# A rank-one term seeded into PSUM by ScalarE, and the doubling of P moved from VectorE to ScalarE

## The chip, the cores and the metric

The kernel runs on one core of a Trainium2 chip. The metric is the device time of one execution in microseconds (us). The time before is 1906.95 us, the median of three runs (1909.23, 1906.95 and 1906.66). The profiled execution took 1907.31 us, with a span of 1905.5 us from the first to the last instruction and a mean granted TensorE clock of 0.999.

## The reference

Two operations follow each other. First an input `x` of 8 x 3008 x 256 is mixed by a two-dimensional Fourier transform, of which the real part is kept. Then the 24,064 rows of 256 go through a two-layer network with a gelu in its quick form:

```python
X = np.fft.fft(np.fft.fft(x, axis=1), axis=2).real      # 8 x 3008 x 256
h = X.reshape(24064, 256) @ w_in                          # 256 x 2048
g = h * (1.0 / (1.0 + np.exp(-1.702 * h)))
out = g @ w_out                                           # 2048 x 256
```

## The kernel before, in words

**The mathematics of a step.** The transform over the 256 columns is folded into the first weights, so that TensorE forms the hidden layer from two real matrices, the cosine part and the sine part of the transform over rows. Two rows of the transform that mirror each other share them: with P the product with the cosine weights (`wcs[0]`), Q' that with the sine weights (`wcs[1]`) and N a rank-one term (a weight per hidden unit, `af2`, times a row of the transform that stands in `nb` on all partitions), the forward rows are N + P + Q' and the mirrored ones N + P - Q'. Row 0 of the sine operands holds the data of N, so the sine product as it stands in the kernel before is Q = Q' + N. `af2` is twice the weights' row, so `af2` times `nb` is 2N.

**Tiling.** The rows of a batch are handled in three blocks, each with two halves (`hh`) of 256 columns, of which the second half of the first block has 226. For each half, eight steps (`p` = 0 to 7, `NP` = 8) go through the 2,048 hidden units, 256 in a step. `steps` has 8 x 3 x 2 x 8 = 384 steps, of 48 in a batch. The first eight (`t < NP`) go by `hidden` and `rows` and are called the forward steps here; the other 376 go by the loop's second branch. The schedule is written out by hand: the loop at L915 to L977 gives the order in which each engine's queue gets its instructions, and `extra` (L869 to L913) puts the next batch's transform (`fold1` on GpSimd, `mix1` and `stage2` on TensorE, their evacuations, loads and stores) into certain steps.

**A step t of the 376.** `x` is one bank of PSUM, `b0` or `b1` in turn.

1. TensorE: `second(t)` adds Q to x (L532); P was put there a step earlier by `begin(t)` (L525). Each is four matmul calls in two column halves and leaves eight records in the profile.
2. TensorE: `product(t - LAG, 0)` and `product(t - LAG, 1)` (L640) multiply the activated rows of three steps ago (`LAG` = 3) by the second weights and add them up in the banks `po`, over the eight steps of a half. Between the two parts stands `begin(t + 1)`, the P of the next step. At the first step of a half (`(t - LAG) % NP == 0`) P comes ahead of all products. The products are of a Strassen-Winograd form: their operands are sums `s` of activated rows (`sums`, L566: two on GpSimd, L576 and L577, two on VectorE, L579 and L580), and one of the products is divided once more (`small_products`, L605, with sums by `deeper`, L586).
3. ScalarE: `middle(t + 2)` writes the rank-one term 2N to an SBUF tile `g` as two activations with a scale per partition (L544). `forward(t)` reads x and writes the gelu of the forward rows (L557). `activate_back(t - 1)` applies the gelu to the mirrored rows of the step before (L564).
4. VectorE: `doubled(t + 1)` reads x of the next step while it holds P alone, and makes g = 2P + 2N (L550). Q of that step may be added only after that. `backward(t)` forms g - x = N + P - Q' in reversed order (L505 in `reversed_sum`).
5. VectorE and ScalarE: every eighth step, `combine`, `combine_small`, `swap` and `combine_last` evacuate the po banks (L699, L705, L708, L728, L736 to L738, L747), transpose (L679) and store.

`spare` lists the PSUM banks that `bank` hands out. In the 376 steps it holds `b{t % 2}` (the bank of x of step t, free after the reversed subtraction) and `b2`; `mix1` and `stage2` take two banks from it. `mix1`'s evacuation is two ScalarE copies (L235), that of `stage2` four VectorE transposes (L340).

Of the kernel before, what the change touches and what calls it, by code (L numbers as in the profile page):

```python
# [43 lines left out]
LAG = 3  # L44
# [67 lines left out]
def kernel(ctx: ExitStack, tc, x, w_in, w_out, tab1, tab2, out):  # L112
# [31 lines left out]
    af2 = const.tile([128, NF], F32, tag="af2", name="af2")  # L144
# [65 lines left out]
    def mix1(b, m):  # L210

        ps = [bank("ps1") for _ in range(2)]
        queues = {}
        for i in (2 * m, 2 * m + 1):
            for r in range(2):
                for c in range(2):
                    rows, o = slice(64 * r, 64 * r + NA), ps[r][64 * c:64 * c + 64, i % 2 * D:(i % 2 + 1) * D]
                    jj, todo = 4 * i + 2 * r + c, queues.setdefault((r, c), [])
                    if jj:
                        todo.append((2, o, mat(w1, jj, rows), xt[rows, 31 - (2 * i + c), :], True, True))  # L220
                        continue
                    for k, c0, c1 in ((0, 0, H + 1), (1, H + 1, D)):
                        for part in range(2):
                            todo.append((1, o[:, c0:c1], mat(w1, ENDS[k + 2 * part], rows), e0[b][:, part, c0:c1], part == 0,
                                         part == 1))

        had = {key: 0 for key in queues}
        while any(queues.values()):
            key = min((key for key in queues if queues[key]), key=lambda key: (had[key], key))
            size, o, w, rhs, first, end = queues[key].pop(0)  # L230
            had[key] += size
            nc.tensor.matmul(o, lhsT=w, rhs=rhs, start=first, stop=end)  # L232

        for r in range(2):
            nc.scalar.copy(free(xt[:], (4 * m + r) * D, [2 * D, 2], [1, D]), free(ps[r][:], 0, [D, 2], [1, D]))  # L235
# [87 lines left out]
    def stage2(b, blk):  # L323
# [5 lines left out]
        for cs in range(2):  # L329
            for h in range(2):  # L330
                for g in range(4):
                    for u in range(NU):
                        rows, at = slice(64 * u, 64 * u + 64), cs * 256 + h * 128
                        nc.tensor.matmul(ps[u][32 * g:32 * g + 32, at:at + 128], lhsT=m[rows, cs, h * RUN:(h + 1) * RUN],  # L334
                                         rhs=t4[rows, 4 * blk:4 * blk + 4, cs * H + 32 * g:cs * H + 32 * g + 32],
                                         start=True, stop=True)
# [119 lines left out]
    def first_row(n):  # L456
# [4 lines left out]
        nc.scalar.copy(af2[:, 4 * n:4 * n + 4], ps[:, 4 * n:4 * n + 4])  # L461

# [24 lines left out]
    def hidden(t):  # L487

        n = width(t)
        pa, pb = bank("pa"), bank("pb")  # L490
        for ps, cs in ((pa, 0), (pb, 1)):
            for i in range(2):
                halves(ps[:, i * 256:i * 256 + n], *operands(t, cs, i), start=True, stop=True)
# [31 lines left out]
    def begin(t):  # L525

        n = width(t)
        x = xb[t] = bank("x", f"b{t % 2}")
        for i in range(2):
            halves(x[:, i * 256:i * 256 + n], *operands(t, 0, i), start=(i == 0), stop=False)  # L530

    def second(t):  # L532
        n = width(t)
        for i in range(2):
            halves(xb[t][:, i * 256:i * 256 + n], *operands(t, 1, i), start=False, stop=True)

    def middle(t):
# [3 lines left out]
        g = gt[t] = sp.tile([128, 512], F32, tag="dif" if t % 2 else "v", name="g")  # L541
        for i in range(2):
            f = 2 * p + i
            nc.scalar.activation(g[:, i * 256:i * 256 + n], nbt[b, blk][:, hh * 256:hh * 256 + n], ACTF.Copy,  # L544
                                 scale=af2[:, f:f + 1])

    def doubled(t):
        n = width(t)
        g = two(gt[t][:], n)
        nc.vector.scalar_tensor_tensor(g, two(xb[t][:], n), 2.0, g, op0=ALU.mult, op1=ALU.add)  # L550
# [89 lines left out]
    def product(t, part):  # L640

        p, n = steps[t][3], width(t)
        if part == 0 and p == 0:
# [16 lines left out]
        todo = plan[:2] if part == 0 else plan[2:]  # L660

        if t >= len(steps) - 2:
            if part == 0:
# [9 lines left out]
        if part and p == 0:  # L673
# [241 lines left out]
    for t in range(n + LAG):  # L915
        if t < NP:
            if t == NP - 2:
                spare[:] = [tag for tag in spare if tag[0] == "o"] + ["b2"]
            hidden(t)
            if t == NP - 1:  # L920
                begin(NP)
            if t == 0:
# [5 lines left out]
            if t >= LAG:  # L928
                for part in range(2):
                    product(t - LAG, part)  # L930
# [5 lines left out]
            if t == NP - 1:  # L936
                for ahead in range(2):
                    middle(NP + ahead)
        else:
            if t < n:  # L940
                if t + 2 < n:
                    middle(t + 2)
                second(t)
            heads = [(product, t - LAG, 0)] + [(begin, t + 1)] * (t + 1 < n)
            for fn, *args in heads[::-1] if t >= NP + LAG and (t - LAG) % NP == 0 else heads:
                fn(*args)
            product(t - LAG, 1)
            small_products(t - LAG, (1, 2, 4, 7))
            small_products(t - LAG - 1, (5, 6, 3))
            if t == NP:  # L950
                activate(t - 1)
            if t < n:
                forward(t)
            if NP < t <= n:
                activate_back(t - 1)
                sums(t - 1, nc.gpsimd)
# [3 lines left out]
        if NP <= t + 1 < n:  # L960
            doubled(t + 1)
        if t >= NP:
# [11 lines left out]
        if t >= NP:  # L974
            spare[:] = [f"b{t % 2}", "b2"]
# [30 lines left out]
```

## Time and profile before

| engine | busy us | share of the span |
|---|---|---|
| TensorE, matmuls | 1881.4 | 99% |
| VectorE | 1540.6 | 81% |
| ScalarE | 877.5 | 46% |
| GpSimd | 789.9 | 41% |

| what | line | count | busy us |
|---|---|---|---|
| P and Q, all matmuls into x | L480 | 6,016 | 766.2 |
| 2N by ScalarE | L544 | 752 | 336.6 |
| 2P + 2N by VectorE | L550 | 376 | 254.9 |
| reversed rows by VectorE | L505 | 440 | 255.9 |
| gelu of the forward rows | L557 | 376 | 221.9 |
| gelu of the mirrored rows | L564 | 376 | 231.5 |

Busy time is the time in which an engine had at least one instruction at work. A matmul's end is modelled and matmuls overlap, so that TensorE's busy time has to be checked against the starts of its matmuls. In the lines of the timeline, the columns are the start in us from the span's start, the duration in us, the engine (PE is TensorE, PEld its weight loads, DVE VectorE, ACT ScalarE, POOL GpSimd, SP the queue of SyncE), the source line, the operation, what it writes and reads, its shape and how many were merged. Square brackets hold the engine's idle time just before it, and who ended it.

### The profile page before, as it was taken

Reading aid. Unit: us, or ns where it says so; the run is one execution under the profiler, and the core shown is the slowest. Engines: PE = TensorE matmul, PEld = TensorE weight load, DVE = VectorE, ACT = ScalarE, POOL = GpSimd, SP = SyncE. Lnnn points to the kernel's source line nnn. Section 1 sums busy time; section 2 is a strip of 40 time slices with the busy share of each in tenths; the row PEclk is TensorE's granted clock in tenths of the full one; section 3 lists DMA queues with packets and bytes.
Section 4 is the critical chain, followed back from the end, with each engine's and each line's share of the span. In section 5 each row is a group of like instructions: output and inputs, shape, how many; then the busy total and the mean of one; then the engine's idle time right before and its main releaser. Section 6 shows DMA issues by size and latency. Waiting matters only on the chain.

```text
span 1905.5 us, 51020 instructions
## 1 busy us (share of the span) xinstructions
PE 1881.4 (99%) x21392; PEld 1360.9 (71%) x21392; DVE 1540.6 (81%) x3011; ACT 877.5 (46%) x1868; POOL 789.9 (41%) x1073
## 2 busy tenths in 40 slices
PE   8999999999999999999999999999999999999998
PEld 5666777777777777777777777777777767777775
DVE  7688878887788877897788878888787888778876
ACT  6644444454445444444444444444444444444442
POOL 4585324643246322563225532365223643233222
PEclk9999999999999999999999999999999999999999
DMA  8732351236221452315513163132720231202201
GB/s 272 176 50 17 90 82 14 49 52 119 18 23 40 71 101 18 51 22 102 63 15 57 22 117 44 22 53 44 113 25 20 18 50 49 27 14 17 27 13 23
DMA packets 145398, 104.92 MB, mean 55 GB/s; under 512 B 104914, under 2 KB 127986, under 8 KB 143984
## 3 DMA queue, kind: packets, MB, share of 16 engines
q1 hardware_dynamic: 143952, 101.14, 31.2%
q8 instruction: 167, 2.74, 0.6%
q10 hardware_dynamic: 1216, 0.52, 0.1%
q14 instruction: 63, 0.52, 0.1%
HBM read 58.38 MB, written 48.01 MB: 56 GB/s over the span
## 4 chain that ended last, share of the span: by engine, by line
PE 88%; DVE 8%; ACT 1%; DMA 1%; issue 1%; POOL 0%; SPq 0%; DVEq 0%; ACTq 0%; POOLq 0%
PE po L480 39%; PE x L480 31%; PE po L625 13%; DVE r L597 2%; PE ps L334 1%; PE ps L232 1%; DVE g L550 1%; DVE s L580 1%; DVE s L579 1%; DVE h L505 1%; DVE c L705 1%; PE ps L285 1%; DVE u L705 1%; DMA wo<-in_tab_dram 0%; PE psw L450 0%
## 5 line engine op out<-in xcount | busy, mean ns | idle before, releaser
L480 PE MATMUL x<-pq,wcs 128*64 128x256 f32 (+1 forms) x6016 | 766.2, 376 | 3.9 <-DVE g L550 3.7
L480 PE MATMUL po<-s,wo 128*64 128x256 f32 (+1 forms) x4512 | 573.0, 375 | 5.6 <-DVE c L705 3.5
L557 ACT ACTIVATE h<-x 128x512 f32<-128x512 f32 (+1 forms) x376 | 221.9, 590 | 761.9 <-PE x L480 610.1
L480 PEld LDWEIGHTS x<-pq,wcs 128*64 128x64 f32 x6016 | 423.3, 137 | 172.8 <-issue 11.6
L576 POOL TENSOR_TENSOR s<-h 128x256 f32<-128x256 f32 (+1 forms) x282 | 207.4, 735 | 742.5 <-issue 614.1
L480 PEld LDWEIGHTS po<-s,wo 128*64 128x64 f32 x4512 | 330.2, 137 | 159.1 <-POOL s L576 9.2
L505 DVE TENSOR_TENSOR h<-g,x 128x512 f32<-128x512 f32 (+2 forms) x440 | 255.9, 593 | 209.5 <-ACT h L557 207.8
L544 ACT ACTIVATE g<-nb,af 128x256 f32<-128x256 f32 (+1 forms) x752 | 336.6, 498 | 2.1 <-DVE h L514 0.9
L550 DVE SCALAR_TENSOR_TENSOR g<-x,g 128x512 f32<-128x512 f32 (+1 forms) x376 | 254.9, 678 | 74.8 <-PE x L480 74.3
L480 PE MATMUL po<-h,wo 128*64 128x256 f32 (+1 forms) x1824 | 264.2, 376 | 1.6 <-DVE u L705 1.4
L564 ACT ACTIVATE h<-h 128x512 f32<-128x512 f32 (+1 forms) x376 | 231.5, 616 | 0.2 <-DVE h L505 0.2
L577 POOL TENSOR_TENSOR s<-h 128x256 f32<-128x256 f32 (+1 forms) x282 | 204.0, 723 | 0.0
L576 POOL TENSOR_TENSOR held<-h 128x256 f32<-128x256 f32 (+1 forms) x94 | 68.0, 723 | 306.7 <-ACT h L564 153.2
L480 PE MATMUL po<-held,wo 128*64 128x256 f32 (+1 forms) x1504 | 193.4, 375 | 0.1
L625 PE MATMUL po<-r,held 128*64 128x128 f32 (+1 forms) x2208 | 185.0, 270 | 0.1
L480 PEld LDWEIGHTS po<-h,wo 128*64 128x64 f32 x1824 | 132.9, 137 | 66.6 <-DVE u L705 7.6
L579 DVE TENSOR_TENSOR s<-s,h 128x256 f32<-128x256 f32 (+1 forms) x282 | 177.5, 629 | 0.1
L597 DVE TENSOR_TENSOR r<-h 128x256 f32<-128x256 f32 (+1 forms) x368 | 162.8, 484 | 0.0
L625 PEld LDWEIGHTS po<-r,held 128*64 128x64 f32 x2208 | 143.0, 137 | 23.3 <-DVE r L597 0.3
L580 DVE TENSOR_TENSOR s<-h,s 128x256 f32<-128x256 f32 (+1 forms) x282 | 147.5, 523 | 9.7
L480 PEld LDWEIGHTS po<-held,wo 128*64 128x64 f32 x1504 | 110.8, 137 | 49.7 <-DVE held L579 0.5
L625 PE MATMUL po<-h,wo 128*64 128x128 f32 (+1 forms) x1472 | 111.9, 270 | 0.0
(106 smaller groups left out, 1717.8 us busy)
## 6 DMA issues: line engine op xcount, KB each, us to landing
out_dram<-os SPq DMA_DIRECT2D x284, 64.0 KB
Td<-xt SPq DMA_DIRECT2D x14, 768.0 KB
t<-Td SPq DMA_DIRECT2D x7, 1536.0 KB
xt<-in_x_dram SPq DMA_DIRECT2D x14, 512.0 KB
xt<-Xr SPq DMA_DIRECT2D x14, 512.0 KB
nb<-pq SPq DMA_DIRECT2D x23, 256.0 KB
out_dram<-os SPq DMA_DIRECT2D x96, 56.0 KB
Xr<-in_x_dram SPq DMA_DIRECT2D x7, 752.0 KB
```

What stands on the lines that cost most here:

```text
L480: nc.tensor.matmul(out[c0:c0 + 64], lhsT=lhs[:, c0:c0 + 64], rhs=rhs, skip_group_check=True, **how)
L505: nc.vector.tensor_tensor(free(h[:], 512 + at + m - 1, [256, 2], [RUN, blocks], [-1, m]), *ins, op=op)
L544: nc.scalar.activation(g[:, i * 256:i * 256 + n], nbt[b, blk][:, hh * 256:hh * 256 + n], ACTF.Copy, scale=af2[:, f:f + 1])
L550: nc.vector.scalar_tensor_tensor(g, two(xb[t][:], n), 2.0, g, op0=ALU.mult, op1=ALU.add)
L557: nc.scalar.activation(two(h[:], n), two(xb[t][:], n), ACTF.Gelu_apprx_sigmoid)
L564: nc.scalar.activation(g, g, ACTF.Gelu_apprx_sigmoid)
L576: eng.tensor_tensor(s1, a21, a22, op=ALU.add)
L577: eng.tensor_tensor(s3, a11, a21, op=ALU.subtract)
L579: eng.tensor_tensor(s2, s1, a11, op=ALU.subtract)
L580: eng.tensor_tensor(s4, a12, s2, op=ALU.subtract)
L597: nc.vector.tensor_tensor(out, i0, i1, op=how)
L625: nc.tensor.matmul(sub(k)[64 * side:64 * side + 64, :w], lhsT=lhs, rhs=rhs, start=(p == 0 and k in (1, 2)), stop=(p == NP - 2), skip_group ...
```

## The change

The rank-one term N is written straight into the bank of x by ScalarE (`middle`, with a new table `af1` = `af2` / 2 for the scale), and P is then added on top by TensorE, which no longer starts a new sum there. The doubling becomes a ScalarE activation that copies 2 x (N + P) to `g`; VectorE's `doubled` goes away. Q is computed with row 0 of the sine weights set to zero (a GpSimd memset of `wcs[1][0:1]`, once, after the forward steps), so that it is Q'. g - x is 2(N + P) - (N + P + Q') = N + P - Q', as before, and VectorE's reversed subtraction is the same instruction.

The order of a step changes with it. `middle(t + 2)` stands at the end of step t, after the reversed subtraction and the gelu of the mirrored rows, both of step t now (the latter and GpSimd's two sums stood one step later). If step t had `mix1` or `stage2` in it (`special`), the bank is still lent out, and `middle` comes in the next step (`after`), ahead of `begin`, which then has four of the products in front of it instead of two (`cut`). In steps that are not special, the extras get `b2` alone. [...]four other places (L220, L224, L336, L493) set their start flag only on the first matmul of a bank; the bank of `hidden` is named for one of the forward steps.

```diff
+    af1, af2 = (const.tile([128, NF], F32, tag=f"af{i}", name=f"af{i}") for i in (1, 2))
...
         nc.scalar.copy(af2[:, 4 * n:4 * n + 4], ps[:, 4 * n:4 * n + 4])
+        nc.scalar.activation(af1[:, 4 * n:4 * n + 4], ps[:, 4 * n:4 * n + 4], ACTF.Copy, scale=0.5)
...
-        pa, pb = bank("pa"), bank("pb")
+        pa, pb = (bank(name, f"b{i}" if t == NP - 3 else None) for i, name in enumerate(("pa", "pb")))
...
+    def middle(t):
+        b, blk, hh, p = steps[t]
         n = width(t)
         x = xb[t] = bank("x", f"b{t % 2}")
         for i in range(2):
-            halves(x[:, i * 256:i * 256 + n], *operands(t, 0, i), start=(i == 0), stop=False)
+            f = 2 * p + i
+            nc.scalar.activation(x[:, i * 256:i * 256 + n], nbt[b, blk][:, hh * 256:hh * 256 + n], ACTF.Copy,
+                                 scale=af1[:, f:f + 1])
+    def begin(t, cs=0):
         n = width(t)
         for i in range(2):
+            halves(xb[t][:, i * 256:i * 256 + n], *operands(t, cs, i), start=False, stop=(cs == 1))
...
     def doubled(t):
         n = width(t)
-        g = two(gt[t][:], n)
-        nc.vector.scalar_tensor_tensor(g, two(xb[t][:], n), 2.0, g, op0=ALU.mult, op1=ALU.add)
+        g = gt[t] = sp.tile([128, 512], F32, tag="dif" if t % 2 else "v", name="g")
+        nc.scalar.activation(two(g[:], n), two(xb[t][:], n), ACTF.Copy, scale=2.0)
...
             if t == NP - 1:
+                middle(NP)
                 begin(NP)
+                nc.gpsimd.memset(wcs[1][0:1, :], 0.0)
...
+            after, special = (any(fn in (mix1, stage2) for fn, _ in extra.get(k, ())) for k in (t - 1, t))
             if t < n:
-                if t + 2 < n:
-                    middle(t + 2)
-                second(t)
-            heads = [(product, t - LAG, 0)] + [(begin, t + 1)] * (t + 1 < n)
-            for fn, *args in heads[::-1] if t >= NP + LAG and (t - LAG) % NP == 0 else heads:
-                fn(*args)
-            product(t - LAG, 1)
+                begin(t, 1)
+            cut = 4 if after else 0 if (t - LAG) % NP == 0 and t >= NP + LAG else 2
+            product(t - LAG, 0, cut)
+            if t < n:
+                if t == NP:
+                    activate(t - 1)
+                forward(t)
+            if t + 1 < n:
+                if after:
+                    middle(t + 1)
+                begin(t + 1)
+            product(t - LAG, cut, None)
             small_products(t - LAG, (1, 2, 4, 7))
             small_products(t - LAG - 1, (5, 6, 3))
-            if t == NP:
-                activate(t - 1)
-            if t < n:
-                forward(t)
-            if NP < t <= n:
-                activate_back(t - 1)
-                sums(t - 1, nc.gpsimd)
             swap(t - LAG - 2)
             if t < n:
                 backward(t)
-        if NP <= t + 1 < n:
-            doubled(t + 1)
-        if t >= NP:
+            if t + 1 < n:
+                doubled(t + 1)
+            if t < n:
+                activate_back(t)
+                sums(t, nc.gpsimd)
+            if t + 2 < n and not special:
+                middle(t + 2)
             sums(t - 2, nc.vector)
...
         if t >= NP:
-            spare[:] = [f"b{t % 2}", "b2"]
+            spare[:] = [f"b{t % 2}"] * special + ["b2"]
```

## The prediction

> **What bounds the kernel now.** I read the page's engine table, then the chain that ended last and the costliest groups, then the timeline. From the page:
>
> ```profile
> PE 1881.4 (99%) x21392; PEld 1360.9 (71%) x21392; DVE 1540.6 (81%) x3011; ACT 877.5 (46%) x1868; POOL 789.9 (41%) x1073
> ...
> PE 88%; DVE 8%; ACT 1%; DMA 1%; issue 1%; POOL 0%; SPq 0%; DVEq 0%; ACTq 0%; POOLq 0%
> ...
> L544 ACT ACTIVATE g<-nb,af 128x256 f32<-128x256 f32 (+1 forms) x752 | 336.6, 498 | 2.1 <-DVE h L514 0.9
> L550 DVE SCALAR_TENSOR_TENSOR g<-x,g 128x512 f32<-128x512 f32 (+1 forms) x376 | 254.9, 678 | 74.8 <-PE x L480 74.3
> ```
>
> TensorE is busy 99% and carries 88% of the chain; the 8% of VectorE is what a change of engines could free. Busy time hides short gaps, so I take start times. One ordinary step, from the timeline (start us, duration, engine, line, tiles, count):
>
> ```profile
> 1000.03 1.03 PE L480 MATMUL x<-pq,wcs 128*64 128x256 f32 x8
> ...
> 1000.89 0.60 PE L480 MATMUL po<-h,wo 128*64 128x256 f32 x4
> ...
> 1001.75 1.03 PE L480 MATMUL x<-pq,wcs 128*64 128x256 f32 x8
> ...
> 1002.62 1.47 PE L480 MATMUL po<-s,wo 128*64 128x256 f32 x12
> ...
> 1004.57 1.03 PE L480 MATMUL x<-pq,wcs 128*64 128x256 f32 x8
> ```
>
> Q (1000.03) to the next group takes 0.86 us for 8 records, 0.1075 each; a record 226 wide takes 0.0955 (0.76 for 8), a small one 0.055. A step is Q 8, P 8, product 20 and 12 or 16 small ones: 3.87 + 0.66 or 0.88, so 4.53 or 4.75. The trace has 4.54 from this Q to the next, and 4.76 to the one after. **Ordinary steps have no idle TensorE to win.** What can be won lies in a few steps of each batch:
>
> ```profile
> 565.33 0.63 DVE L550 SCALAR_TENSOR_TENSOR g<-x,g 128x452 f32<-128x452 f32 x1 [0.22 <-PE x L480]
> ...
> 567.26 1.73 PE L480 MATMUL x<-pq,wcs 128*64 128x226 f32 x16
> ...
> 568.54 0.94 DVE L705 TENSOR_TENSOR u<-u,po 128x256 f32<-128x256 f32 x2
> ...
> 569.01 0.60 PE L480 MATMUL po<-h,wo 128*64 128x226 f32 x4
> ...
> 569.52 0.69 DVE L705 TENSOR_TENSOR c<-u,po 128x512 f32<-128x512 f32 x1
> ...
> 570.35 1.37 PE L480 MATMUL po<-s,wo 128*64 128x226 f32 x12 [0.35 <-DVE c L705]
> ...
> 582.02 0.62 DVE L550 SCALAR_TENSOR_TENSOR g<-x,g 128x452 f32<-128x452 f32 x1
> ...
> 582.69 0.41 PE L480 MATMUL x<-pq,wcs 128*64 128x226 f32 x2 [0.50 <-DVE g L550]
> ```
>
> Sixteen records of 0.0955 from 567.26 end their turn at 568.79; the products begin at 569.01, those into the second bank at 570.35, where 569.55 was due: 0.80 lost to VectorE, which reads the old po banks late. At 582.69 Q is 0.67 late for the late 2P. In the same way 0.76 goes at 607.4 to 608.6. That is 2.23 us a batch; the pattern stands six times (from 338, 569, 799, 1030, 1261 and 1491). The first batch has its own: 1.25 near 141 to 184, about 1.9 at 115 to 125. Three more waits, at 559, 790 and 1252, make 0.5.
>
> **What the Trainium skill says.** "TensorE: Matmul & The Clock Gate", section "Wait — 56ns, not 53.3ns?", puts starts at the width over 2.4 GHz plus 2.5 ns, 109 ns for 256; the 0.1075 agrees, so this TensorE is at its rate. "PSUM — Partial Sum Buffer", section "PSUM bank collisions raise a hardware error", wants any two engines kept apart by bank. The trace agrees: the reversed subtraction (L505) waits 207.8 us in all for the gelu (L557), though both only read x. "SBUF — State Buffer", section "Who interferes with whom", makes a VectorE operation with two SBUF inputs and a GpSimd operation shut each other out; here L580 takes 0.43 at 1004.09, and 0.80 at 566.51 beside GpSimd's L207. The removed L550 has one SBUF input; taking it away frees its time, not that port.
>
> **The change part by part.**
> *Removed from VectorE:* 376 x 678 ns, 255 us: 81% becomes 67%. Only where VectorE is behind does it count. Before the late reads above, one L550 (0.63) goes from the chain 565.3 to 569.0; the 0.22 and the 0.37 of the first banks vanish, the 0.52 becomes some 0.1 (u 0.94 and c 0.69 still lie between), the 0.33 vanishes. The 0.67 vanishes, since 2P no longer queues behind transposes and sums.
> *2P on ScalarE:* 376 more. Price: the nearest rows are L557 (PSUM in, 598 ns) and L495 (copy, 582); "ScalarE: Activation LUTs", section "What ACT_TABLE_LOAD costs", gives 186 + 0.833 x 512 = 613. I take 600, ends 580 and 613: 226 us, ScalarE to about 1,100 us (58%). In a step (us after Q starts): Q ends 0.9, gelu to 1.6, P ends 2.7, 2P to 3.3, second gelu to 3.9, the two row copies to 4.8. Q of the next step wants 2P at 4.5 (1.2 spare); P wants the row at 4.5 + 1.73 = 6.2 (1.4 spare), or 5.4 where the products come second (0.6 spare). So it lies beside TensorE in ordinary steps.
> *Row copies into PSUM:* the same 752 activations of 498 ns, not more. Written to PSUM they may be quicker; ends 450 and 502, I take 498. What is new is that P waits for them. They wait for the reversed subtraction of the step two before (same bank), which the second gelu ahead of them in ScalarE's queue waits for anyway. Queued behind that gelu are the row, the first gelu of the next step and, where a tile ends, the two copies L699 and L708.
> *After mix1 and stage2:* there the bank is lent out, and the row comes only in the step after, between gelu and P, with four products ahead of P instead of two. ScalarE after a mix1, before:
>
> ```profile
> 592.19 1.08 PE L480 MATMUL x<-pq,wcs 128*64 128x256 f32 x8
> ...
> 592.35 1.07 ACT L235 COPY xt<-ps 128x512 f32<-128x512 f32 x2 [3.40 <-PE ps L232]
> ...
> 593.31 0.92 ACT L544 ACTIVATE g<-nb,af 128x256 f32<-128x256 f32 x2
> ...
> 594.12 0.60 ACT L557 ACTIVATE h<-x 128x512 f32<-128x512 f32 x1
> ```
>
> From Q's start: copies until 1.12, then gelu 0.48 (they overlap a little), then 0.92 for the two rows: 2.52, P at 2.57 with 0.05 for the semaphore. TensorE is there at Q + four products: 0.76 + 1.53 = 2.29 (both 226 wide; rows then end at 2.42), 0.86 + 1.53 = 2.39, or 0.86 + 1.73 = 2.59. Two of the four mix1 of a batch so cost about 0.18, two nothing: 0.36 x 6 and 0.18 in the first batch, 2.3 us. The other bound: if 498 were 450, 1.1; if copies or semaphores take 0.2 more, 28 x 0.2 = 5.6 on top. After stage2 the VectorE transposes free the bank near 1.05, before the gelu ends (1.4): nothing.
> After P, 2P must end before Q again: P to 3.6, 2P to 4.25; TensorE is ready at 2.57 + 0.86 + 0.43 + 0.66 = 4.52. With the three half copies (L736 to L738, 1.27 in all) queued ahead of 2P, still 4.25 against 4.39. Free, but barely.
> *The second gelu* moves from after the next step's first gelu to its own step, GpSimd's sums (0.73 each) with it, some 2 us earlier. On GpSimd the folds for the next mix1 now queue behind sums that wait for that gelu: they end some 2 us later, about 1.5 us before mix1 needs them. The products use those sums three steps later. Nothing. No DMA moves; SP's queue keeps its order.
> *Start:* four more copies of 4 columns (a L461, not on the chain); a row-0 memset on GpSimd, about 2 us by L793 (1.01 for 1,024 columns), after the last forward matmuls at 81.6, needed by Q at 86.4, beside 3.5 us of products. P there waits for its row, 0.4; the 0.44 that Q loses at 86.41 to L550 goes: even, within 1. The flags at L220, L232, L336, L493 change no work.
>
> *Sum*, against the span of 1905.5: 6 x 2.23 + 1.25 + 0.5 = 15.1, of 115 to 125 half, 1.0, less 6 x 0.1, less 2.3: 13.2, rounded to 13. The span becomes 1892.5. The profiled run took 1907.31, the three timed 1906.66, 1906.95 and 1909.23; against the median, 1894.
>
> **The rivals.**
> *The evacuation stays late.* The first copy of po (L699) now stands behind the row, which stands behind the second gelu, which waits for VectorE. If that ends the chain, the 0.80 and 0.76 stay, and 6 x 0.67 + 1.2 - 2.3 = 3 is won: 1904. For it: ScalarE becomes a queue with VectorE in it. Against: the copy is due at 4.6 to 5.1, so the first read ends 1.1 into the next step, and TensorE comes at 1.5 or 1.7.
> *The steps after mix1 and stage2 cost more*, 0.25 at each of 51 (28 + 23) against 2.3 in all: 12.8 - 2.3, so 1904.5. For it: spare of 0.14. Against: measured durations fit.
> *Slower: ScalarE closes a ring.* Place: Q waits for 2P, which waits behind a ScalarE queue that waits for VectorE. It decides when gelu, 2P, second gelu and rows lag more than 1.2 us further than the 4.8 above; then every step grows. With 0.1 over in 376 steps, 37.6 lost against 15 won: 1907 + 22 = 1929. Against: 2.7 us of ScalarE in 4.6, VectorE with 0.68 less a step.
> *The seed does not do what it says* (P overwriting the row) would change the values, and no time.
>
> **How the numbers follow.** The forecast 1894 has 0.72, within 1889 (every loss gone, quicker rows) and 1899 (slow copies). The late evacuation 0.11, at 1904; the dear steps 0.10, at 1899 to 1907; the ring 0.05; anything else 0.02. What a measurement can tell from no change is about 0.2%, 3.8 us: faster is under 1903.1, slower above 1910.8. Faster: 0.72, half of the next two, 0.83; same 0.10; slower 0.07 with the unknown. The range reaches into the two middle cases: 1889 to 1904.
>
> **What would show it.** Right: VectorE near 67%, ScalarE near 58%; TensorE's waits for L705 and 2P gone; Q starts 4.54 and 4.76 apart in ordinary steps. After a mix1, P may wait for the row up to 0.2. Wrong: ordinary steps longer than 4.76, idle of TensorE ended by ScalarE beyond 6 us in all, or products at a tile's start that still wait for VectorE's reads.

## The result and the profile after

| kernel | median us | range | runs | profiled span |
|---|---|---|---|---|
| before | 1908.09 | 1906.66 to 1909.70 | 4 | 1905.5 |
| after | 1899.88 | 1898.17 to 1900.84 | 4 | 1897.2 |

After over before is 0.9956, 95% interval 0.9939 to 0.9973. The change gains 8.2 us; the forecast was a gain of 13. By the interval the gain lies between 5 and 12 us, so that it is clear of zero and short of the forecast. In the code of after the lines are: matmuls L481, row copies L533, 2P L545, forward gelu L552, mirrored gelu L559, reversed subtraction L506, GpSimd's sums L571 and L572, VectorE's sums L574, L575 and L592. The page of after, its engine table, chain and two groups (count, busy us, mean ns):

```profile
PE 1879.8 (99%) x21392; PEld 1364.9 (72%) x21392; DVE 1210.5 (64%) x2635; ACT 1117.5 (59%) x2248; POOL 786.7 (41%) x1074
...
PE 93%; POOL 3%; ACT 1%; DVE 1%; DMA 1%; issue 1%; SPq 0%; POOLq 0%; DVEq 0%
...
L545 ACT ACTIVATE g<-x 128x512 f32<-128x512 f32 (+1 forms) x376 | 222.0, 590 | 341.3 <-PE x L481 340.1
...
L533 ACT ACTIVATE x<-nb,af 128x256 f32<-128x256 f32 (+1 forms) x752 | 352.9, 469 | 13.2 <-DVE pq L340 1.0
```

VectorE's share of the chain falls from 8% to 1%. It lost 330 us of busy time, not 255: its sums with two inputs in SBUF are shorter too, which the experiments take up. A row copy takes 469 ns on average to PSUM where it took 498 to SBUF. Next the timeline of after at the tile's start that lost 0.80 us before, at 567 there:

```profile
564.37 1.70 PE L481 MATMUL x<-pq,wcs 128*64 128x226 f32 x16
...
564.65 0.94 DVE L700 TENSOR_TENSOR u<-u,po 128x256 f32<-128x256 f32 x2
...
565.63 0.69 DVE L700 TENSOR_TENSOR c<-u,po 128x512 f32<-128x512 f32 x1
...
565.89 0.55 PE L481 MATMUL po<-h,wo 128*64 128x226 f32 x4
...
566.27 1.70 PE L481 MATMUL po<-s,wo 128*64 128x226 f32 x16
```

The first read of the old banks begins 0.28 us after Q instead of 1.28, and the products run on from 565.89 to 566.27 without a gap. So it is at every tile's start, and Q no longer waits for 2P. Both kernels run the same number of matmuls, so the 8.3 us between the spans must lie in the time that TensorE loses between them. To find what stands in the place of the old waits I took, place by place, the time between the starts of TensorE's matmuls less what their widths account for. Three kinds of loss are new or larger.

**P waits for its row.** There are 19 waits of 0.20 to 0.22 us, 4.0 us in all: two per batch after a mix1, and one after a stage2, which was priced at nothing (the first batch has one alone). The timeline of after at a wait that follows a stage2:

```profile
555.30 0.83 DVE L592 TENSOR_TENSOR r<-h,r 128x256 f32<-128x256 f32 x1
...
556.06 1.43 DVE L340 STREAM_TRANSPOSE pq<-ps 128x256 f32<-128x256 f32 x4
...
556.92 0.94 ACT L533 ACTIVATE x<-nb,af 128x226 f32<-128x226 f32 x2 [0.16 <-DVE pq L340]
...
557.91 0.58 PEld L481 LDWEIGHTS x<-pq,wcs 128*64 128x64 f32 x8 [0.47 <-ACT x L533]
```

The transposes that free the bank begin only when VectorE's last sum ends, at 556.1, so the row begins 0.16 later than ScalarE could have written it. (The weight loads run ahead of the matmuls: of their 0.47 the matmuls lose 0.2.)

**TensorE's instructions are not there.** In the first mix1 of two batches TensorE stops with no engine to wait for. From its first matmul to that of the next Q this mix1 takes 1.45 us in the last four batches, but 2.94 at 338 us and 3.03 at 569: 1.5 and 1.6 lost. The line behind the second stop:

```profile
570.69 0.32 PE L232 MATMUL ps<-e,w 47*64 47x127 f32 x1 [1.37 <-issue]
```

The page lists the queue q8 "instruction" with 169 packets of 2.77 MB, 16 KB each. The view of the DMA queues of after, cut to 552 to 568.3 us, lists no packet of it; cut to 568.3 to 569.4, it lists one:

```profile
q1 hardware_dynamic: 377, 0.38, 99.9%
q8 instruction: 1, 0.02, 5.6%
```

TensorE resumes at 570.69, 1.3 us after that. The Trainium skill ("Runtime: NRT & Kernel Launch", section "Instruction fetch mechanics") says that instructions come in blocks of 16 KiB, 256 of them, which the sequencer fetches over a DMA queue of its own, and that the crossing is mostly hidden. The size agrees (169 x 256 is 43,264, against 2 x 21,392 matmuls and weight loads, so these are TensorE's); at three of the 169 blocks the hiding failed by more than 1 us. The third place is at 250 us, where after loses 1.8 us, counted over the matmuls around the stop. The kernel before has only that one, 2.3 us at 253.

**GpSimd is full in the first batch.** One stop of 1.99 us at 122; the timeline of after:

```profile
121.57 0.87 POOL L572 TENSOR_TENSOR s<-h 128x226 f32<-128x226 f32 x1
...
122.40 0.87 POOL L207 TENSOR_TENSOR xt<-xt 111x254 f32<-111x254 f32 x1
123.23 0.72 POOL L208 TENSOR_TENSOR xt<-xt 111x254 f32<-111x254 f32 x1
...
124.01 0.44 PE L232 MATMUL ps<-xt,w 47*64 47x256 f32 x3 [1.78 <-POOL xt L208]
```

mix1 waits for a fold that stands behind the moved sums. GpSimd is busy for 11.84 of the 12 us from 112 to 124, in before as in after.

### The profile page after: what moved, and what is told of

Read it like the earlier page. It is cut to its first block, busy times and chain, and to the rows that moved or that the text cites. A ratio compares the mean times of both kernels' runs of the same rounds, so it can differ in the third digit from the quotient of the medians.

```text
span 1897.2 us, 51367 instructions
## 1 busy us (share of the span) xinstructions
PE 1879.8 (99%) x21392; PEld 1364.9 (72%) x21392; DVE 1210.5 (64%) x2635; ACT 1117.5 (59%) x2248; POOL 786.7 (41%) x1074
## 3 DMA queue, kind: packets, MB, share of 16 engines
q8 instruction: 169, 2.77, 0.6%
## 4 chain that ended last, share of the span: by engine, by line
PE 93%; POOL 3%; ACT 1%; DVE 1%; DMA 1%; issue 1%; SPq 0%; POOLq 0%; DVEq 0%
PE po L481 42%; PE x L481 33%; PE po L620 14%; PE ps L232 2%; PE ps L334 1%; DMA raw<-in_moe_w_in_dram 1%; POOL wo L444 1%; PE psw L450 1%; ACT xt L235 0%; DMA wo<-in_tab_dram 0%; POOL held L633 0%; POOL wst L426 0%; ACT x L533 0%; POOL s L572 0%; DVE m L412 0%
## 5 line engine op out<-in xcount | busy, mean ns | idle before, releaser
L481 PE MATMUL x<-pq,wcs 128*64 128x256 f32 (+1 forms) x6016 | 765.7, 377 | 1.0 <-ACT x L533 0.2
L506 DVE TENSOR_TENSOR h<-g,x 128x512 f32<-128x512 f32 (+2 forms) x440 | 257.7, 598 | 535.2 <-ACT h L552 534.8
L481 PE MATMUL po<-s,wo 128*64 128x256 f32 (+1 forms) x4512 | 568.6, 375 | 1.3 <-issue 1.3
L481 PEld LDWEIGHTS x<-pq,wcs 128*64 128x64 f32 x6016 | 420.2, 137 | 175.1 <-ACT x L533 18.6
L571 POOL TENSOR_TENSOR s<-h 128x256 f32<-128x256 f32 (+1 forms) x282 | 206.4, 732 | 790.4 <-ACT h L559 771.8
L481 PEld LDWEIGHTS po<-s,wo 128*64 128x64 f32 x4512 | 332.0, 137 | 148.4 <-issue 1.7
L545 ACT ACTIVATE g<-x 128x512 f32<-128x512 f32 (+1 forms) x376 | 222.0, 590 | 341.3 <-PE x L481 340.1
L552 ACT ACTIVATE h<-x 128x512 f32<-128x512 f32 (+1 forms) x376 | 221.4, 589 | 273.2 <-PE x L481 267.8
L533 ACT ACTIVATE x<-nb,af 128x256 f32<-128x256 f32 (+1 forms) x752 | 352.9, 469 | 13.2 <-DVE pq L340 1.0
L481 PE MATMUL po<-h,wo 128*64 128x256 f32 (+1 forms) x1824 | 262.0, 376 | 0.0
L559 ACT ACTIVATE h<-h 128x512 f32<-128x512 f32 (+1 forms) x376 | 231.3, 615 | 32.9 <-DVE h L506 31.7
L572 POOL TENSOR_TENSOR s<-h 128x256 f32<-128x256 f32 (+1 forms) x282 | 205.9, 730 | 0.0
L481 PE MATMUL po<-held,wo 128*64 128x256 f32 (+1 forms) x1504 | 192.4, 375 | 0.0
L571 POOL TENSOR_TENSOR held<-h 128x256 f32<-128x256 f32 (+1 forms) x94 | 76.4, 812 | 257.0 <-ACT h L559 243.5
L481 PEld LDWEIGHTS po<-h,wo 128*64 128x64 f32 x1824 | 133.8, 137 | 60.0
L592 DVE TENSOR_TENSOR r<-h 128x256 f32<-128x256 f32 (+1 forms) x368 | 165.5, 491 | 0.0
L481 PEld LDWEIGHTS po<-held,wo 128*64 128x64 f32 x1504 | 110.8, 137 | 48.7
L574 DVE TENSOR_TENSOR s<-s,h 128x256 f32<-128x256 f32 (+1 forms) x282 | 127.7, 453 | 0.0
L575 DVE TENSOR_TENSOR s<-h,s 128x256 f32<-128x256 f32 (+1 forms) x282 | 121.0, 429 | 9.6
```

The costliest lines, as they stand in the source:

```text
L481: nc.tensor.matmul(out[c0:c0 + 64], lhsT=lhs[:, c0:c0 + 64], rhs=rhs, skip_group_check=True, **how)
L506: nc.vector.tensor_tensor(free(h[:], 512 + at + m - 1, [256, 2], [RUN, blocks], [-1, m]), *ins, op=op)
L533: nc.scalar.activation(x[:, i * 256:i * 256 + n], nbt[b, blk][:, hh * 256:hh * 256 + n], ACTF.Copy, scale=af1[:, f:f + 1])
L545: nc.scalar.activation(two(g[:], n), two(xb[t][:], n), ACTF.Copy, scale=2.0)
L552: nc.scalar.activation(two(h[:], n), two(xb[t][:], n), ACTF.Gelu_apprx_sigmoid)
L559: nc.scalar.activation(g, g, ACTF.Gelu_apprx_sigmoid)
```

## The experiments

All ratios are to runs of before on the same chip, and no kernel leaves out a part of the work. Where a place in a trace is named, it is that of the one profiled execution. The edits are against after, unless another is named.

### The two moves to ScalarE's queue, apart

E1 puts the doubling back on VectorE and leaves the rest.

```diff
-        nc.scalar.activation(two(g[:], n), two(xb[t][:], n), ACTF.Copy, scale=2.0)
+        nc.vector.tensor_scalar(two(g[:], n), two(xb[t][:], n), scalar1=2.0, scalar2=None, op0=ALU.mult)
```

> The doubling of x goes back to VectorE (a multiplication by 2 from PSUM to SBUF); the seed by ScalarE, the zeroed row and the new order of the step stay. Theory A, the gain is VectorE's shorter queue: VectorE goes up by some 376 x 0.6 to 0.68 us, 225 to 255 us, to about 77%, the three places where TensorE waited for VectorE in each batch (first and second bank of the products at a tile's start, Q behind 2P) come back, up to 2.2 us a batch, and the time is 1905 to 1914. Theory B, the gain is the new order of the step (the second gelu and GpSimd's sums a step earlier, the seed): the time stays within 1898 to 1902, and the waits stay away although VectorE is as busy as that.

Measured: 1968.35 us, ratio 1.0307 (1.0292 to 1.0321). Both theories missed it by 50 us or more. The engine table of E1, then lines of its waits (total us, times, longest):

```profile
PE 1905.0 (97%) x21392; PEld 1369.3 (70%) x21392; DVE 1718.3 (87%) x3011; ACT 929.9 (47%) x1872; POOL 851.1 (43%) x1074
```

```profile
ACT h L559 <- DVE h L506: 463.2, 300, 3.6
...
PEld x L481 <- DVE g L545: 33.7, 47, 1.6
...
PE x L481 <- DVE g L545: 22.8, 39, 1.3
```

In the new order the mirrored gelu stands in ScalarE's queue behind VectorE's reversed subtraction, and the row and the next forward gelu stand behind that gelu. With VectorE loaded, VectorE waits for ScalarE and ScalarE for VectorE, and Q for 2P. That is a ring like the one of the prediction's slower rival, only that here 2P stands on VectorE. E5 and E6 therefore put the gelu (and GpSimd's sums with it) back in its old place, one step later, E5 with the doubling on ScalarE and E6 with it on VectorE as in E1.

```diff
+            if NP < t <= n:
+                activate_back(t - 1)
+                sums(t - 1, nc.gpsimd)
             swap(t - LAG - 2)
...
-            if t < n:
-                activate_back(t)
-                sums(t, nc.gpsimd)
```

> As after, but the mirrored rows' gelu and GpSimd's two sums stand one step later again, behind the next step's forward gelu, as they stood before; the doubling stays on ScalarE. Theory A (the doubling's move alone brings the gain, the gelu's earlier place nothing): within 1.5 us of 1899.9; the 2 us gap of TensorE at 122 us shrinks to under 0.7, since GpSimd's folds there no longer queue behind the sums; VectorE's two-input sums take longer again, 500 to 640 ns in place of some 450, beside GpSimd's sums at their old place, and VectorE's total grows by 40 to 80 us. Theory B (the gelu's place is needed for the gain, since the row copies ahead of it or behind it come late): 1903 or more, with waits of P or Q for ScalarE in many steps.

> As e5_gelu_back, with the doubling done by VectorE besides. Theory A (the 60 us of e1_double_on_vector came from the ring of queues: the mirrored rows' gelu, which waits for VectorE, stands in front of the row copies and the next gelu on ScalarE): with that gelu back in its old place most of it goes, 1902 to 1912. Theory B (it came from VectorE's own load, 87%, whatever the order): 1940 or more still.

Measured: E5 1911.45 us, ratio 1.0009 (1.0003 to 1.0016), theory B by its time, and by its waits only in part: GpSimd's stop at 122 went as theory A had it, but VectorE's total grew by 306 us, not 40 to 80; E6 1921.98, ratio 1.0068 (1.0054 to 1.0081), between its two theories. In E6 the row copies still wait 131.7 us in all for the reversed subtraction, and Q up to 1.0 us for a 2P that VectorE makes late. As a table of ratios:

| | gelu in its old place | gelu in its own step |
|---|---|---|
| doubling on VectorE | 1.0068 (E6) | 1.0307 (E1) |
| doubling on ScalarE | 1.0009 (E5) | 0.9956 (after) |

The gelu's move costs 46 us with the doubling on VectorE and wins 10 with it on ScalarE. The two terms of the prediction don't add: each is worth what the other makes of it. E6 also shows a price that no term had: it has all of the change but these two moves, the seed by ScalarE above all, and is 13 us slower than before. The two moves together win 21.

What E5 loses shows on VectorE. Its engine table, and one group of the page in E5 and in after:

```profile
PE 1888.3 (99%) x21392; PEld 1346.7 (70%) x21392; DVE 1516.1 (79%) x2635; ACT 1118.7 (59%) x2248; POOL 907.4 (47%) x1074
...
L575 DVE TENSOR_TENSOR s<-h,s 128x256 f32<-128x256 f32 (+1 forms) x282 | 227.2, 806 | 9.6
```

```profile
L575 DVE TENSOR_TENSOR s<-h,s 128x256 f32<-128x256 f32 (+1 forms) x282 | 121.0, 429 | 9.6
```

VectorE gave up 255 us of doubling and is busy only 24 us less than before. The timeline of an ordinary step of E5, then that of after:

```profile
1010.80 1.00 POOL L571 TENSOR_TENSOR s<-h 128x256 f32<-128x256 f32 x1 [2.73 <-issue]
...
1011.25 0.84 DVE L575 TENSOR_TENSOR s<-h,s 128x256 f32<-128x256 f32 x1
...
1011.76 0.91 POOL L572 TENSOR_TENSOR s<-h 128x256 f32<-128x256 f32 x1
...
1012.01 0.95 DVE L592 TENSOR_TENSOR r<-r,h 128x256 f32<-128x256 f32 x1
```

```profile
1003.12 0.42 DVE L575 TENSOR_TENSOR s<-h,s 128x256 f32<-128x256 f32 x1
...
1003.46 0.42 DVE L592 TENSOR_TENSOR r<-r,h 128x256 f32<-128x256 f32 x1
...
1003.91 0.42 DVE L592 TENSOR_TENSOR r<-h,r 128x256 f32<-128x256 f32 x1
...
1004.41 0.72 POOL L571 TENSOR_TENSOR s<-h 128x256 f32<-128x256 f32 x1 [3.13 <-ACT h L559]
```

VectorE's sums take 0.84 and 0.95 us beside GpSimd's and 0.42 alone, and GpSimd's take 0.9 to 1.0 in place of 0.72. It agrees with the Trainium skill, "SBUF — State Buffer", section "Who interferes with whom", as the prediction cites it. In after GpSimd's sums begin just when VectorE's end; in E5 they coincide. In each batch after the first, TensorE then stops again at a tile's start: for 0.43 us until VectorE has read a bank, and for 0.33 in another tile until a GpSimd sum is there. It also stops for 0.40 and 0.18 for a 2P that stands behind the swap copies and the gelu. Waits of TensorE in E5:

```profile
PE po L481 <- DVE c L700: 1.6, 6, 0.3
PE x L481 <- ACT g L545: 1.4, 6, 0.2
PE po L481 <- POOL s L571: 1.1, 7, 0.2
```

(These count the idle time alone; counted by starts, as above, six batches lose 4.6 us to the late sums and reads and 3.5 to the late 2P. So waits for late sums and waits for ScalarE's order are both in E5's loss.)

E10 tries to remove only the collision: E5 with VectorE's sums ahead of its reversed subtraction.

```diff
+            sums(t - 2, nc.vector)
+            deeper(t - 2, 0)
+            deeper(t - 3, 1)
             swap(t - LAG - 2)
             if t < n:
                 backward(t)
...
-            sums(t - 2, nc.vector)
-            deeper(t - 2, 0)
-            deeper(t - 3, 1)
```

> e5_gelu_back with VectorE's sums (two of sums, those of deeper) ahead of its reversed subtraction in each step instead of behind it, so that they run while it waits for the forward gelu and not beside GpSimd's sums. Theory A (e5's loss of some 11 us is those sums colliding with GpSimd's): VectorE's total falls from 1516 to 1210 to 1280 us, its two-input sums to 430 to 500 ns, and the time to 1898 to 1903. Theory B (the loss is the gelu's place in ScalarE's queue): VectorE's total falls, the time stays at 1907 or more.

Measured, theory B by the numbers: 1915.38 us, ratio 1.0041 (1.0025 to 1.0056); VectorE 1384.7 us, L575 526 ns. Of the 306 us that VectorE has in E5 over after, 131 went, and the time grew. The waits of E10 name a new one:

```profile
PE ps L232 <- DVE h L506: 8.9, 14, 0.7
```

The reversed subtraction is later, and mix1 wants the bank that it reads. So the edit had a price of its own, and the run doesn't tell how E5's loss divides between collision and ScalarE's order.

### The late instruction blocks

E2 moves the copy of the batch after next (`turn`, 1.5 MB, in the same queue as the broadcast of the row of N and right behind it) sixteen steps on. E7 leaves it and splits the broadcast (256 KB, L348) into two halves, three steps apart.

```diff
-            at(t0 + 10, turn, b + 2)
+            at(t0 + 26, turn, b + 2)
```

```diff
-            nc.sync.dma_start(out=nb[:], in_=free(row, 0, [0, 128], [1, 512]))
+            nc.sync.dma_start(out=nb[:, at:at + 256], in_=free(row, at, [0, 128], [1, 256]))
...
                 at(t0 + blk * NF + 9, nyquist, *nxt)
+                at(t0 + blk * NF + 12, nyquist, *nxt, 1)
```

> The large copy from DRAM to DRAM for the batch after next (7 us of DMA at a busy share near 0.9) is issued 16 steps later in a batch, step 26 instead of 10. Theory A, the two gaps of 1.3 and 1.6 us inside the first mix1 of the second and third batch (338 and 569 us), which no engine ended, are TensorE's instructions arriving late behind that copy: both go, about 2.9 us less, 1896.5 to 1897.5, unless a fetch collides at the new place, where a like gap would then stand. Theory B, they are GpSimd's late folds, as the gap of 1.8 us at 122 us is by the profile: both stay at 1.3 and 1.6, and the time is 1899 to 1901.

> As after, but the broadcast of the row of N over the partitions goes as two transfers of 128 KB, three steps apart, in place of one of 256 KB. Theory A (the gaps of TensorE near 338 and 569 us are instruction blocks that come late behind that broadcast, 8 us long): both shrink below 0.4, 1896.5 to 1898.5, and nothing else changes. Theory B (other transfers, or the place in the block sequence, delay the fetch): the gaps stay at 1.0 or more, 1899 to 1901. Theory C (the second half, three steps later, meets another fetch): the gaps move by 10 to 15 us and keep their size.

Measured: E2 1900.56 us, ratio 0.9953 (0.9942 to 0.9965). The first mix1 of the two batches takes 2.26 and 2.64 us, so that 0.8 and 1.2 are lost instead of 1.5 and 1.6. The time is theory B's, the gaps are neither's. The turn was not what held the block: E3 and E4 below, which leave it in its place, lose 0.9 and 1.0, and 1.2 and 0.8. (With another pace the loss is another: E6 and E10, with the whole broadcast too, lose 0.4 at most.) In that stretch the DMA engines are busy but move next to nothing; the view by windows of after, then of E2, which has no turn there (length, then busy time and instructions of each engine, clock, DMA share, GB/s):

```profile
560.00:564.00 4.00, 4.00 (x46) 2.95 (x44) 2.50 (x6) 2.85 (x8) 3.15 (x5) 1.00 0.90 27
564.00:568.00 4.00, 4.00 (x50) 3.15 (x48) 3.72 (x9) 2.40 (x6) 2.61 (x4) 1.00 0.82 35
```

```profile
560.00:564.00 4.00, 4.00 (x46) 3.10 (x48) 2.06 (x7) 2.36 (x5) 1.74 (x4) 1.00 0.79 26
564.00:568.00 4.00, 4.00 (x52) 3.10 (x50) 3.79 (x9) 2.82 (x7) 3.33 (x5) 1.00 0.88 27
```

That is the broadcast. In after it is issued at 557.6, just ahead of the turn, as the timeline has it:

```profile
557.55 0.53 SPq L348 DMA_DIRECT2D nb<-pq  x1
558.12 7.48 SPq L171 DMA_DIRECT2D Xr<-in_x_dram  x2
```

E7 took 1897.97 us, ratio 0.9947 (0.9934 to 0.9959), and both gaps are gone: the first mix1 takes 1.45 us in both batches, as it does in E9 and E11, which have the halves too. TensorE's blocks start to arrive at 553.0, 565.9 and 572.0 us in place of 550.3, 568.3 and 572.4. The distance from the broadcast says more: in these two batches of after, E2 and before the block begins 10.4 to 10.9 us after the whole broadcast was issued, and in E7 5.6 and 5.7 us after the first half was. So the block comes about when the broadcast is through. In before too: but there the last block had come 3.5 and 3.8 us ahead of the broadcast, in after 7.2 and 6.1, and before does not run out. That is theory A for the place. For the time the interval overlaps after's; the whole gain of 3.1 us is seen only in the trace, which loses 1.7 elsewhere to a lower clock (last section).

### The row after mix1

E3 puts the row ahead of the forward gelu in every step after a mix1 or stage2. E9 does so only after mix1 and has E7's halves. E8 does so only after mix1 as well, without the halves, and moves the three swap copies behind the doubling. The edit of E3, then that of E8 (of which E9 has the first part):

```diff
+                if after and t + 1 < n:
+                    middle(t + 1)
                 forward(t)
             if t + 1 < n:
-                if after:
-                    middle(t + 1)
                 begin(t + 1)
```

```diff
+            mixed = any(fn is mix1 for fn, _ in extra.get(t - 1, ()))
...
+                if mixed:
+                    middle(t + 1)
                 forward(t)
...
-                if after:
+                if after and not mixed:
                     middle(t + 1)
...
-            swap(t - LAG - 2)
...
                 doubled(t + 1)
+            swap(t - LAG - 2)
```

> In the steps after a mix1 or a stage2 ScalarE writes the row into x ahead of the first gelu, not after it. Theory A, P waits there for the row at the end of ScalarE's chain copies, gelu, row: the 19 waits of TensorE of 0.20 to 0.22 us go, 4 us less, 1895.5 to 1897. Theory B, P waits for the bank itself (mix1's copies or stage2's transposes) or for the semaphore: the waits stay, 1899 to 1901. Theory C, the later first gelu makes the reversed subtraction and so the second gelu and 2P late: new waits of Q for 2P, above 1901.

> As after, but in the step after a mix1 the row's two copies stand ahead of the forward gelu (in the step after stage2 behind it, as in after), and the three half copies of swap stand behind the doubling. Theory A (the waits of P after mix1 are those copies' place in ScalarE's queue, and the 0.19 us waits of Q that a row put first brings are the swap copies ahead of 2P): 13 waits of 0.2 us and the ones of Q gone, 1896.5 to 1898, TensorE's idle time ended by ScalarE under 2 us. Theory B (what is moved behind the doubling delays the last combination and the next half's banks): new waits of TensorE at the first steps of a half, 1899 to 1902.

> e7_broadcast_halves, and in the step after a mix1 (not after stage2) the row's two copies stand ahead of the forward gelu; the swap copies stay where they are in after. Theory A (the 0.21 us waits of P after a mix1 are the place of the copies, and e8's loss was the swap copies alone, which pushed the second gelu and the row back): two waits of P a batch gone, at most one wait of Q of 0.19 in their place, 1 to 2 us below e7, 1896 to 1897. Theory B (the row ahead of the gelu delays the forward gelu and with it the tile's reads, so that the next banks come late): waits of 0.5 at the second bank of a tile as in e3_row_first, 1898 to 1899.

Measured: E3 1898.76 us, ratio 0.9943 (0.9928 to 0.9958), not to be told from after. The waits after mix1 went and new ones came: 0.52 us at the second bank of a tile's start, since VectorE's chain behind the later forward gelu is late (Q begins at 566.24 and `u` at 567.26, 1.0 us after it, where after has 0.28), and 0.19 of Q for 2P. The waits after stage2 stayed, at 0.23 us or more, as its theory B has it. E8 1907.55, ratio 0.9993 (0.9985 to 1.0002): a loss of 8 us against after that neither theory had. Its timeline at one of the new waits:

```profile
154.06 0.38 ACT L733 COPY held<-held 64x226 f32<-64x226 f32 x1
...
154.46 0.63 ACT L559 ACTIVATE h<-h 128x512 f32<-128x512 f32 x1
...
155.00 0.97 ACT L533 ACTIVATE x<-nb,af 128x256 f32<-128x256 f32 x2
...
156.02 1.08 PE L481 MATMUL x<-pq,wcs 128*64 128x256 f32 x8 [0.48 <-ACT x L533]
```

Ahead of the doubling the three copies lie in the time that ScalarE waits for P anyway. Behind it they push gelu and row back, and P loses 0.65 and 0.92 us at two places of each batch. E9 took 1894.83 us, ratio 0.9932 (0.9919 to 0.9944), theory A and 1 to 2 us better than it expected: of the waits after mix1, 0.19 of Q a batch is left; those after stage2, which it leaves alone, are still 0.21 in five batches.

### The first batch, and before without such gaps

E4 starts the first batch's folds a step earlier. E11 instead adds two shifts to E9: the first mix1 a step later, and the load of a batch of x (`load_x`, 3 MB, issued from 233 to 239 us) eight steps later. E12 is before with E11's three shifts that are no part of the change (halves, mix1, load).

```diff
-                    at(t0 + 7 + 2 * c + part + late, fold1, b + 1, c, part, nc.gpsimd)
+                    at(t0 + 7 + 2 * c + part + late - (b == 0), fold1, b + 1, c, part, nc.gpsimd)
```

```diff
-                    at(t0 + 9 + 2 * c + late, mix1, b + 1, c // 2)
+                    at(t0 + 9 + 2 * c + late + (b == 0 and c == 1), mix1, b + 1, c // 2)
...
-                at(t0 + 33 + late, load_x, b + 2)
+                at(t0 + 33 + 3 * late, load_x, b + 2)
```

> In the first batch alone GpSimd's folds are issued one step earlier. Theory A, the gap of 1.8 us inside the first mix1 at 122 us is the fold that now queues behind sums that wait for the second gelu: it goes, about 1.8 us less, 1897.5 to 1898.5. Theory B, GpSimd is full there (weights' differences, sums and folds), and only the order of its work changes: the gap shrinks by less than 0.5 us or another wait for GpSimd's sums takes its place, 1899 to 1901.

> e9_halves_row_after_mix1 with two places of the first batch shifted: its first mix1 one step later (the folds ahead of it stay), and the load of the batch after next eight steps later, away from the broadcast near 245 us. Each place is read by itself in the trace. Theory A: the 2.0 us gap at 123 us goes, since the fold it waited for ends 4.6 us before it then, and with it the half clock after it; the gap of 2.7 us at 251 goes, since the instruction block that came late there stood behind that load: 1890 to 1892.5. Theory B: GpSimd is full there and the next mix1 waits instead, or the load delays the block at its new place near 260 to 280 us: 1893.5 to 1896, with gaps of 1 us or more in other places before 300 us.

> The kernel before with the three shifts that are no part of the change: the broadcast in halves, the first batch's first mix1 one step later and its load eight steps later. The kernel after with the same three is e11 less the row's earlier place after mix1, some 3 us (e7 to e9), so about 1894.5. Theory A (late instruction blocks and the full GpSimd in the first batch took part of what the change freed, since they stand in other places in the kernel before): before gains little, its one gap of 2.4 us at 253 and some of the four waits between 118 and 125, 1904.5 to 1906.5, and the change is worth 10 to 12 us between kernels without such gaps. Theory B (such gaps cost both kernels alike, and the change was worth 8 from the first): before gains some 5 to 6 as after does, 1901.5 to 1904.

Measured: E4 1899.83 us, ratio 0.9950 (0.9937 to 0.9963), theory B: nothing won. The gap at 122 went, and one of 0.99 came at 116, where VectorE's sums now wait 2.33 us for GpSimd: another order within a full GpSimd only moved the wait. E11 1891.42, ratio 0.9904 (0.9887 to 0.9920), theory A and the fastest of all, below before and after with intervals apart. The largest gap between 85 and 325 us is 0.33, and where after has one block at 247.8 after a pause of 19.6 us, E11 has two, at 240.7 and 248.2. E12 1906.92, ratio 0.9994 (0.9985 to 1.0002). Chain and waits of E12:

```profile
PE 87%; DVE 9%; DMA 2%; ACT 1%; issue 1%; POOL 1%; SPq 0%; DVEq 0%; POOLq 0%; ACTq 0%
```

```profile
PE x L482 <- DVE g L552: 5.1, 9, 1.2
...
PE po L482 <- DVE c L707: 3.5, 14, 0.4
```

Before gains some 1 us (0 to 3) from the three shifts, of which the last two alone gave E11 3.4: theory A, and a little less than it expected. The stop at 253 is gone from E12's trace, but the waits for VectorE are all there. By their ratios E12 and E11 are 17 us apart, by their medians 15.5, of which E9's row after mix1 is about 3 (E7 to E9, whose intervals overlap). Between kernels without these gaps the change itself is so worth some 12 to 14 us. This is an estimate from differences of runs; the kernel after with the three shifts alone was not run.

## Why the prediction was right, and short by five

- **What TensorE would win:** right. The waits for the late reads and for 2P, taken as 2.23 us a batch (2.1 when counted again), are gone from all six patterns; the 0.1 a batch that was to stay went too. Ordinary steps stay at 4.54 and 4.76.
- **ScalarE's price:** right. 2P took 590 ns where 600 was taken, ScalarE is at 59% where 58% was forecast, and the row took 469 ns, within 450 to 502.
- **P waits for its row after mix1 and stage2:** the term of 2.3 us measured 4.0. After mix1 the wait is 0.21 instead of 0.18; after stage2 "nothing" was 0.20 a batch, since the term took VectorE to be free at the transposes, and its sums of the step before stand ahead of them.
- **The wins of 115 to 125 (1.0 counted):** nothing was won there: 2.0 us are lost in after as about 1.9 were before. "On GpSimd the folds for the next mix1 now queue behind sums" was the right mechanism, and its "about 1.5 us before mix1 needs them" is false in the first batch, where GpSimd has next to no idle time.
- **What no term had:** the late instruction blocks, 3.1 us lost at 338 and 569, 0.6 won at 250. A faster TensorE meets the same transfers at another place of its instruction stream.

Together 13.2 - 1.7 - 1.0 - 3.1 + 0.6 is 8.0, and the span moved by 8.3. This is closer than it can be trusted: kernels that are the same program up to there (after, E2, E3, E4, E7, E8, E9 and E11) reach the first P on a seeded row anywhere from 80.8 to 83.4 us, and after's trace is the earliest. E7 shows the late blocks by themselves; E9 and E11 give back in time what the rows after mix1, the first batch and the load took.

The time was inside the stated range by some luck. The forecast's own case had 1889 to 1899, and 1899.88 lies just outside it, in the part of the range that the two middle rivals had added. Neither of those rivals accounts for the time.

- **The second gelu: "Nothing".** This was the largest error, and it didn't show in the sum. The forecast took VectorE from 81% to 67% by taking 255 us away, and after's 64% looks like it; but E5, with the gelu in its old place, frees only 24 us and is no faster than before. It took the gelu's move to turn the doubling's move into time. In the traces that move brings GpSimd's sums out of the way of VectorE's and 2P ahead of the gelu in ScalarE's queue; which of the two counts for more is not shown (E10). The prediction named the interference and said that the removed instruction "frees its time, not that port", and did not look where the other sums would then fall. The seed itself, taken as free but for P's wait, is part of E6's 13 us.
- **The rivals:** evacuation and dear steps at 1904 didn't come; of the second's 10.5 us, 1.7 are there. The ring, given 0.05, is near: moving the doubling back to VectorE (E1) is enough to close one, at 60 us above before.

## What to carry to other kernels

When work leaves an engine, ask what its next instructions will then coincide with: of two moves that look separate, here one alone costs 46 us, the other alone wins 11, and both together win 21 (E6 to E1, E6 to E5, E6 to after). In a queue that works in order, put work that nobody waits for ahead of a wait that comes anyway, not behind it (E8). When a gain is smaller than its sum, look for "issue" gaps and for the instruction packets in the view of the DMA queues before doubting the sum.

## What was not expected of the hardware

- TensorE can run out of instructions behind ordinary transfers. The stops here are of up to 3.2 us, behind a broadcast of 256 KB that keeps the DMA engines 0.8 to 0.9 busy at some 27 GB/s, and behind a load. Their length varies from trace to trace (at 250 us 1.8 in after, 2.5 in E4, 3.2 in E9). In the two batches that stop, a block comes 10 to 11 us after the whole broadcast was issued, and 5.6 or 5.7 after a half of it. Why the queues serve it only then was not settled; halving one transfer and moving another removed the stops.
- After the stop of 2 us at 122, which has only sparse mix1 work around it, the clock granted to TensorE fell to half for 3.4 us in some traces (E2, E3, E7 and E9; in E8 for 6.8) and not in after. Windows of E9, which hold both clocks:

```profile
124.00:128.00 4.00, 3.08 (x26) 1.99 (x28) 0.00 (x0) 2.08 (x5) 3.56 (x6) 0.83 0.00 0
128.00:132.00 4.00, 4.00 (x40) 2.84 (x38) 2.09 (x5) 1.36 (x3) 0.00 (x0) 0.74 0.01 4
```

  Matmul records start in pairs (the 0.1075 of the prediction is the mean over such a pair). In this stretch the pairs are some 0.18 us too far apart, nine times: 1.7 us. The Trainium skill ("TensorE: Matmul & The Clock Gate", section "Part 1: The HAM clock gate") names an idle window of about 3.4 us for this; here 2 us and thin work were enough. The length of the stop does not decide it: E9's 3.2 us at 254, amid full work, left the clock at 1.00, while E5's 2.2 at 254, amid full work too, was followed by half the clock. E11, without the stop at 122, has a clock of 1.00 there.
